# Loading 128 rows of wo first, halving w_down's first loads, and storing y with one DMA, in a one-token decode kernel

## The chip, the cores and the metric

The kernel runs on one core of a Trainium2 chip. The metric is the device time of one execution in microseconds (us), the median of several runs, so lower is better. A profiled execution also gives a span, from its first to its last instruction, which is about 2 us shorter than the run's time. All positions below, such as "at 287.5", are microseconds from the start of that span. In the profile lines PE is TensorE and PEld its weight loads, DVE is VectorE, ACT ScalarE, POOL GpSimd and SP SyncE; SPq and ACTq are the instruction sequencers of SyncE and ScalarE, and q1, q8, q10 and q14 are queues of transfers.

## The reference

One decoded token for a batch of two: attention over the last 2048 of 8192 cached keys, then a gated feed-forward block. Everything is bf16.

```python
B, D, Hq, Hkv, Sk, Dh, F = 2, 640, 32, 32, 8192, 192, 1536
W = min(4096, max(256, Sk // 4))                       # 2048
q = (layernorm(x) @ wq)                                # 32 heads of 192
k, v = k_cache[:, :, Sk - W:, :], v_cache[:, :, Sk - W:, :]
o = softmax(q @ k.T * Dh ** -0.5) @ v                  # per batch row and head
h = x + o.reshape(B, 1, Hq * Dh) @ wo
hn = layernorm(h)
y = h + (gelu(hn @ w_gate) * (hn @ w_up)) @ w_down
```

Every input byte that is needed is read once: 100.66 MB of K and V, 7.86 MB each of wq and wo, 5.90 MB of w_gate, w_up and w_down. That is the 122.29 MB that the profile counts on SyncE's queue. The output is 2,560 bytes.

## The kernel before

All large loads go out on SyncE's queue, in the order in which they are needed, into one ring of on-chip memory. A load waits only until the part of the ring that it overwrites has been read. ScalarE's queue carries x at the start and half of the result at the end.

```python
WDC = ((0, 3), (3, 6), (6, 9), (9, 11), (11, 12))   # w_down: five loads, of 3, 3, 3, 2, 1 row groups
...
    P.op("sp", lambda e, v=v, src=src: e.dma_start(v, src), W=toks + [("sem", sem)], dma=sem)   # every ring load
...
def load_wo(J):                                     # four quarters of wo, the last one in two parts
    src = A_wo[1536 * J:1536 * (J + 1), :].rearrange("(p kk) n -> p kk n", kk=12)
    for i, (k0, k1) in enumerate(wo_parts(J)): ...
def wo_parts(J):
    return ((0, 12),) if J < 3 else ((0, 8), (8, 12))
...
P.op("act", lambda e: e.dma_start(xrow[0:2, :], A_x[:, 0, :]), W=["xrow"], dma="dx")
load_k(0); load_wq(); load_k(1); ...                # then v0, k2, v1, ..., wo quarters between,
load_wo(2); load_wo(3); load_ffn()                  # w_gate, w_up in two parts, w_down in five
```

The tail of the arithmetic:

```python
# w_gate and w_up: four column blocks side by side on the PE, contiguous columns
    e.matmul(bank[32*r:32*r+2, 0:384], lhsT=hnT[:, c, :], rhs=wv[:, c-c0, 384*r:384*(r+1)], ...)
...
gT = ffn_columns(grow, "grow", tps[0], 0)
pe(h_rows, ...)                                     # puts h into the accumulator of y
... # gelu of the gate on DVE and ScalarE, w_up, product -> uT
for i, (f0, f1) in enumerate(WDC):                  # w_down, group by group as it lands
    e.matmul(m1[32*r:32*r+2, 0:160], lhsT=uT[:, f, :], rhs=wd[:, f-f0, 160*r:160*(r+1)], ...)
dve(lambda e: e.tensor_copy(yrow[0:98, :], m1[0:98, 0:160]), ...)
for b, q in ((0, "sp"), (1, "act")):                # result: one store for each batch row, on two queues
    P.op(q, lambda e, b=b: e.dma_start(out[b, 0, :].rearrange("(r n) -> r n", r=4), yrow[b:b+97:32, :]), ...)
```

SyncE waits for both stores; then the program ends.

## Time and profile before

| | before |
|---|---|
| median of the first 3 runs | 294.56 us (294.52 to 294.61) |
| profiled span | 292.5 us |
| SyncE's queue q1 | 98.0% of 16 engines' span |
| last w_down load, first / mean / last of its 16 completions | 287.45 / 288.44 / 289.52 |
| stores issued, later one complete | 290.27, 292.12 |

The two bottom rows come from the records of single transfers. A load is spread over 16 transfer engines and completes once on each, so "first" and "last" are the fastest and the slowest engine. The prediction quotes the page's rates, the windows at both ends and the chain of waits. Here is what it uses but doesn't print: first the page's line of busy engines and its line of packets.

```profile
PE 192.4 (66%) x2141; PEld 149.2 (51%) x2141; DVE 128.0 (44%) x310; ACT 96.0 (33%) x120; POOL 8.4 (3%) x35
DMA packets 6654, 122.44 MB, mean 419 GB/s; under 512 B 754, under 2 KB 884, under 8 KB 1652
```

PE, the busiest engine, works 66% of the span; 122.44 MB is what all queues move together, instructions included. Then lines of the timeline (start, duration, engine, source line, operation, tiles, count; in brackets how long the engine was idle before, and what ended that).

```profile
0.74 0.56 ACTq L406 DMA_DIRECT2D xrow<-in_A_x_dram  x1
0.74 0.65 SPq L343 DMA_DIRECT2D ring<-in_A_k_cache_dram  x1
...
280.64 1.77 PE L780 MATMUL sps<-ring,hnT 128*2 128x384 bf16 x20 [0.79 <-DVE hnT L404]
...
283.76 0.71 PE L797 MATMUL m<-hrow,hsel 98*2 98x160 f32 x8
...
284.25 1.82 PE L780 MATMUL ops<-ring,hnT 128*2 128x384 bf16 x20
...
287.46 0.18 DVE L404 TENSOR_TENSOR uT<-tps,ga 128x24 bf16<-128x24 f32 x1 [1.73 <-PE tps L789]
```

Both queues issue their first load at the same moment. The 20 matmuls of w_gate take 1.77 us, the h_rows matmuls (L797) stand right before those of w_up, and uT, which every w_down matmul needs, starts to be written at 287.46.

### The profile page before, as it was taken

Reading aid. Unit: us, or ns where it says so; the run is one execution under the profiler, and the core shown is the slowest. Engines: PE = TensorE matmul, PEld = TensorE weight load, DVE = VectorE, ACT = ScalarE, POOL = GpSimd, SP = SyncE. Lnnn points to the kernel's source line nnn. Section 1 sums busy time; section 2 is a strip of 40 time slices with the busy share of each in tenths; the row PEclk is TensorE's granted clock in tenths of the full one; section 3 lists DMA queues with packets and bytes.
Section 4 is the critical chain, followed back from the end, with each engine's and each line's share of the span. In section 5 each row is a group of like instructions: output and inputs, shape, how many; then the busy total and the mean of one; then the engine's idle time right before and its main releaser. Section 6 shows DMA issues by size and latency. Waiting matters only on the chain.

```text
span 292.5 us, 5066 instructions
## 1 busy us (share of the span) xinstructions
PE 192.4 (66%) x2141; PEld 149.2 (51%) x2141; DVE 128.0 (44%) x310; ACT 96.0 (33%) x120; POOL 8.4 (3%) x35
## 2 busy tenths in 40 slices
PE   2450858848678198849495596658696856586665
PEld 1440436718475195628282575456565653563432
DVE  5950085623437154516155255426265454162331
ACT  2150115623432143616152144324343443341000
POOL 3000020000000000000000000000000000000000
PEclk9996699995979579988879599959797999597955
DMA  7998999999999999999999999999999999999993
GB/s 283 450 497 351 429 437 432 430 432 430 429 415 441 430 430 428 430 430 430 430 412 446 430 430 434 430 430 430 430 430 430 430 430 430 430 430 409 429 404 151
DMA packets 6654, 122.44 MB, mean 419 GB/s; under 512 B 754, under 2 KB 884, under 8 KB 1652
## 3 DMA queue, kind: packets, MB, share of 16 engines
q1 hardware_dynamic: 6632, 122.29, 98.0%
q8 instruction: 7, 0.11, 0.2%
q14 instruction: 3, 0.02, 0.0%
q10 hardware_dynamic: 12, 0.00, 0.0%
HBM read 122.29 MB, written 0.00 MB: 418 GB/s over the span
## 4 chain that ended last, share of the span: by engine, by line
DMA 75%; PE 20%; SPq 3%; DVE 1%; issue 0%
DMA ring<-in_A_k_cache_dram 57%; PE tps L551 15%; DMA ring<-in_A_wq_dram 10%; DMA ring<-in_B_w_down_dram 8%; SPq L343 3%; PE tps L572 2%; PE ops L653 1%; PE m L704 1%; PE m L686 1%; DVE ktr L563 0%; DVE ering L404 0%; PE m L826 0%; PE m L637 0%; PE m L667 0%; DVE yrow L832 0%
## 5 line engine op out<-in xcount | busy, mean ns | idle before, releaser
L551 PE MATMUL tps<-identf,ring 128*128 128x128 f32 x768 | 112.7, 314 | 46.6 <-DMA ring<-in_A_k_cache_dram 45.3
L551 PEld LDWEIGHTS tps<-identf,ring 128*128 128x128 f32 x768 | 104.1, 164 | 50.2 <-DMA ring<-in_A_k_cache_dram 46.6
L560 ACT ACTIVATE ktr<-tps 128x1024 bf16<-128x1024 bf16 x80 | 79.2, 1023 | 83.6 <-PE tps L551 83.6
L563 DVE COPY ktr<-tps 128x1024 bf16<-128x1024 bf16 x112 | 74.2, 688 | 72.2 <-PE tps L551 71.5
L628 ACT ACTIVATE eexp<-sm,nm 128x512 bf16<-128x512 f32 x16 | 11.5, 721 | 65.0 <-DVE nm L626 65.0
L653 PE MATMUL ops<-ring,ering 128*32 128x384 bf16 x512 | 24.9, 339 | 5.4 <-DMA ring<-in_A_v_cache_dram 5.4
L617 DVE CUSTOM_DVE_ANT_1 sm<-sps,mska 128x512 f32<-128x512 f32 x16 | 11.1, 691 | 35.7 <-PE sps L609 35.7
L609 PE MATMUL sps<-ktr,rq 128*16 128x512 bf16 x384 | 24.6, 389 | 1.1 <-POOL rq L404 1.1
L653 PEld LDWEIGHTS ops<-ring,ering 128*32 128x32 bf16 x512 | 12.8, 99 | 14.1 <-DMA ring<-in_A_v_cache_dram 6.7
L609 PEld LDWEIGHTS sps<-ktr,rq 128*16 128x16 bf16 x384 | 9.2, 88 | 11.4 <-POOL rq L404 1.2
L624 PEld LDWEIGHTS m<-mrhs,pm 128*128 128x128 bf16 x16 | 1.5, 96 | 23.5 <-DVE mrhs L400 23.5
L624 PE MATMUL m<-mrhs,pm 128*128 128x16 bf16 x16 | 2.9, 183 | 15.7 <-DVE mrhs L400 15.7
L572 PE MATMUL tps<-ring,xnT 128*32 128x384 bf16 x80 | 5.6, 464 | 11.0 <-DMA ring<-in_A_wq_dram 11.0
L404 POOL TENSOR_TENSOR rq<-qs,mask 128x96 bf16<-128x96 bf16 x16 | 5.6, 360 | 195.4 <-PE sps L609 161.3
L572 PEld LDWEIGHTS tps<-ring,xnT 128*32 128x32 bf16 x80 | 3.1, 132 | 13.3 <-issue 11.2
L595 DVE CAST qs<-ops 128x384 bf16<-128x384 f32 x1 | 0.6, 558 | 17.6 <-PE ops L590 17.6
L404 DVE TENSOR_TENSOR ering<-m,mask 128x256 bf16<-128x256 f32 x16 | 6.7, 418 | 1.9 <-PE m L637 1.7
L456 ACT ACTIVATE lt<-m,eps_t 128x2 f32<-128x2 f32 x2 | 0.5, 262 | 19.4 <-PE m L454 19.4
L579 ACT ACTIVATE qrow<-tps 128x768 bf16<-128x768 f32 x1 | 0.8, 810 | 15.6 <-PE tps L572 15.6
L637 PE MATMUL m<-sel,eexp 128*128 128x64 bf16 x64 | 4.6, 196 | 1.2 <-ACT eexp L628 1.2
L404 DVE TENSOR_TENSOR orow<-m,wm 128x1536 bf16<-128x1536 f32 x3 | 5.3, 1751 | 0.0
L704 PE MATMUL m<-ring,ot 128*2 128x320 bf16 x96 | 4.1, 298 | 1.6 <-DMA ring<-in_A_wo_dram 1.6
(115 smaller groups left out, 86.5 us busy)
## 6 DMA issues: line engine op xcount, KB each, us to landing
ring<-in_A_k_cache_dram SPq DMA_DIRECT2D x16, 3072.0 KB, 31.7
ring<-in_A_v_cache_dram SPq DMA_DIRECT2D x16, 3072.0 KB, 27.3
ring<-in_A_wq_dram SPq DMA_DIRECT2D x1, 7680.0 KB, 28.2
ring<-in_A_wo_dram SPq DMA_DIRECT2D x3, 1920.0 KB, 19.2
ring<-in_B_w_gate_dram SPq DMA_DIRECT2D x1, 1920.0 KB, 32.0
ring<-in_B_w_up_dram SPq DMA_DIRECT2D x1, 1536.0 KB, 24.3
ring<-in_B_w_down_dram SPq DMA_DIRECT2D x3, 480.0 KB, 26.4
ring<-in_A_wo_dram SPq DMA_DIRECT2D x1, 1280.0 KB, 26.8
```

The costliest lines, as they stand in the source:

```text
L343: P.op("sp", lambda e, v=v, src=src: e.dma_start(v, src), W=toks + [("sem", sem)], dma=sem)
L404: return lambda e: e.tensor_tensor(out=out, in0=a, in1=b, op=op)
L551: ins = e.transpose(tps[bi][:, 128 * u:128 * (u + 1)], kv[:, off:off + 128], identf[:, :])
L560: act(lambda e, dst=dst, bv=bv: e.activation(out=dst, in_=bv, func=ACT.Copy), W=[("kt", n)], X=[("t", bi)])
L563: dve(lambda e, dst=dst, bv=bv: e.tensor_copy(dst, bv), W=[("kt", n)], X=[("t", bi)], cls=0)
L572: ins = e.matmul(tps[0][32 * r:32 * (r + 1), 0:384], lhsT=xnT[:, c, 32 * J:32 * (J + 1)], rhs=wq[:, c, 1536 * J + 384 * r:1536 * J + 384 * ...
L609: ins = e.matmul(sps[32 * ch:32 * ch + 16, :], lhsT=rq[:, g % 4, k, :], rhs=ktr[:, k // 2, 1024 * ch + k % 2:1024 * (ch + 1):2], start=(k ...
L617: dve(lambda e: e.tensor_tensor_reduce(out=sm[:, :].rearrange("p (u x) -> p u x", u=4), in0=sps[:, :].rearrange("p (u x) -> p u x", u=4), ...
L628: act(lambda e: e.activation(out=eexp[:, :], in_=sm[:, :], func=ACT.Exp, bias=nm[:, 0:1], scale=1.0, accum_out=zr[:, g % 4:g % 4 + 1]), R= ...
L637: ins = e.matmul(o, lhsT=eexp[:, 128 * u:128 * (u + 1)], rhs=sel64[:, :], start=True, stop=True)
L653: ins = e.matmul(ops_[32 * r:32 * (r + 1), 0:384], lhsT=ering[:, g % 4, t, :], rhs=vv[:, 384 * t:384 * (t + 1)], start=(g % 4 == 0 and t < 4),
L704: ins = e.matmul(m1[32 * r:32 * r + 2, 192:512], lhsT=ot[:, kk, :], rhs=wo[:, kk - k0, 320 * h:320 * (h + 1)], start=(kk == 1 or J < 2 and ...
```

## The change

The intent is to shorten the stream of transfers at its two ends. While SyncE's queue starts up, ScalarE's queue already fetches the last 128 rows of wo, which then need not be loaded near the end. w_down needs one load fewer, with larger packets. And the result leaves in one DMA of 8 rows. The larger w_down rows alter which row of w_down stands on which partition, so w_gate's and w_up's columns are read with a stride; and for one store the two batch rows must lie on partitions 16 apart, so the stationary operand becomes 17 columns wide.

```diff
-WDC = ((0, 3), (3, 6), (6, 9), (9, 11), (11, 12))
+WDC = ((0, 6), (6, 9), (9, 11), (11, 12))
+WOE = 6016
 ... (new tile wosp; wider ot, hsel and uT)
 def load_wo(J):
-    src = A_wo[1536 * J:1536 * (J + 1), :].rearrange("(p kk) n -> p kk n", kk=12)
+    nk = 12 if J < 3 else 11
+    src = A_wo[1536 * J:1536 * J + 128 * nk, :].rearrange("(p kk) n -> p kk n", kk=nk)
-    return ((0, 12),) if J < 3 else ((0, 8), (8, 12))
+    return ((0, 12),) if J < 3 else ((0, 8), (8, 11))
 ... (w_down read as "(q p s) n -> q p s n" with s=6)
+P.op("act", lambda e: e.dma_start(wosp[32:96, :, :], A_wo[WOE:, :].rearrange("(p j) n -> p j n", j=2)), W=["wosp"], dma="dsp")
 P.op("act", lambda e: e.dma_start(xrow[0:2, :], A_x[:, 0, :]), W=["xrow"], dma="dx")
 ... (two memsets on POOL: all of uT, and wosp[0:32])
 ... (oproj(3): four matmuls of wosp, ahead of the wait for the rest of that quarter)
-    rhs=wv[:, c - c0, 384 * r:384 * (r + 1)]
+    cols = wv[:, c - c0, 768 * (r // 2):768 * (r // 2 + 1)].rearrange("p (x s) -> p x s", s=6)
+    rhs=cols[:, :, 3 * (r % 2):3 * (r % 2) + 3]
+pe(h_rows, ...)
 gT = ffn_columns(grow, "grow", tps[0], 0)
-pe(h_rows, ...)
-    m1[32 * r:32 * r + 2, 0:160], lhsT=uT[:, f, :]
+    m1[32 * r:32 * r + 17, 0:160], lhsT=uT[:, f, 0:17]
-dve(lambda e: e.tensor_copy(yrow[0:98, :], m1[0:98, 0:160]), W=["y"], X=["m1"])
-for b, q in ((0, "sp"), (1, "act")):
-    P.op(q, lambda e, b=b: e.dma_start(out[b, 0, :].rearrange("(r n) -> r n", r=4), yrow[b:b + 97:32, :]),
-         R=["y"], W=[("out", b)], dma=f"dout{b}")
+dve(lambda e: e.tensor_copy(yrow[0:113, :], m1[0:113, 0:160]), W=["y"], X=["m1"])
+P.op("act", lambda e: e.dma_start(out[:, 0, :].rearrange("b (r n) -> r b n", r=4), yrow[0:113:16, :]), R=["y"], W=["out"],
+     dma="dout")
```

## The prediction

> **What bounds the kernel now.** I read the page from part 2 down. It says first whether the transfers ever stop.
>
> ```profile
> DMA  7998999999999999999999999999999999999993
> q1 hardware_dynamic: 6632, 122.29, 98.0%
> q8 instruction: 7, 0.11, 0.2%
> DMA 75%; PE 20%; SPq 3%; DVE 1%; issue 0%
> ```
>
> The first line cuts the 292.5 us span into 40 slices and shows the transfer engines at 90% or more in all but the first slices and the last. SyncE's queue (q1) alone fills 98.0% of the span on all 16 engines and moves 122.29 MB; the last line, the chain of waits, is three quarters transfer. Away from the ends the rate is steady at about 430 GB/s. The PE is 66% busy and is not the bound. So the end is set by **start of the transfers + bytes over rate + what follows the last landing**. To move it, a change has to move one of those three.
>
> The start and the end need a finer view. This is a table of short stretches, with the DMA share and GB/s in the last two columns:
>
> ```profile
> 1.60:1.70 0.10, 0.00 (x0) 0.00 (x0) 0.04 (x1) 0.10 (x1) 0.10 (x2) 1.00 0.04 13
> 2.00:2.10 0.10, 0.00 (x0) 0.00 (x0) 0.10 (x1) 0.10 (x1) 0.10 (x1) 1.00 0.00 0
> 2.10:2.20 0.10, 0.00 (x0) 0.00 (x0) 0.10 (x1) 0.10 (x1) 0.10 (x1) 1.00 3.55 983
> 287.00:288.00 1.00, 0.72 (x15) 0.42 (x17) 0.18 (x1) 0.00 (x0) 0.00 (x0) 0.50 0.66 240
> 288.00:289.20 1.20, 1.11 (x36) 0.73 (x32) 0.00 (x0) 0.00 (x0) 0.00 (x0) 0.50 0.33 126
> ```
>
> A packet is booked where it starts, hence 3.55 and 983. ScalarE's tiny load of x starts moving at 1.68 us, but the first packets of K, issued at the same moment, start only at 2.16 to 2.58 us. There is an almost empty half microsecond at the front. At the back the share falls from 1.0 to 0.66 and 0.33: the 16 engines don't finish together. The trace has one completion per engine; those of the last w_down load run from 287.45 to 289.52 us, so the slowest engine, 2.07 us behind the first, sets the end. Then the chain of waits closes with:
>
> ```profile
> 265.46 23.65 DMA ring<-in_B_w_down_dram
> 289.12 0.04 issue
> 289.16 0.73 PE m L826 x12
> 289.89 0.02 issue
> 289.92 0.32 DVE yrow L832
> ```
>
> The PE was idle for 0.44 us before row groups 9 and 10 and for 0.30 us before group 11, both times waiting for w_down: the arithmetic is ahead of the loads at the end. After that, in the order of time:
>
> ```profile
> 290.27 0.66 SPq L834 DMA_DIRECT2D out_dram<-yrow  x1
> 290.27 0.61 ACTq L834 DMA_DIRECT2D out_dram<-yrow  x1
> ```
>
> The store issued by ScalarE completes at 291.94, the one by SyncE at 292.12; SyncE waits for both and the span ends 0.4 us later.
>
> **What the Trainium skill says.** (1) "DMA: Bandwidth & Descriptors", section "Issuing engines are not separate DMA queues": loads issued from ScalarE and SyncE run on the same 16 engines and interleave. So the second queue buys no bandwidth. The trace agrees that a single queue already fills the engines (98.0%). (2) Same page, section "The descriptor swizzle": partitions map to engines in blocks of four, with the halves 0-63 and 64-127 on engines 0-7 and 8-15. Partitions 32-95 in 16 shares of four then follow that same map, which explains the odd range. No run here shows it yet. (3) "SBUF — State Buffer", section "Door 1: The DMA port swizzle (why `[64,N]` ≈ `[32,N]`)": strided reads are free while at least two of the accesses fall in one 16-byte line, 8 bf16 apart at most. The new reads of w_gate and w_up take 3 columns of every 6, so about 4 per line, and should be free; the trace before has only contiguous ones there. (4) "Runtime: NRT & Kernel Launch", section "Instruction fetch mechanics": instructions are refilled in 16 KiB blocks. The trace agrees: seven packets of 16384 bytes on q8, about 1 us each, which compete with the loads.
>
> **The change, part by part.**
>
> *128 rows of wo first.* 128 x 640 x 2 bytes = 0.164 MB. At 430 GB/s that is **0.38 us** of all engines; per engine 4 packets of 2560 bytes, which took about 0.10 us each where w_down uses this size. The bytes leave the second part of the last wo load (landing at 275.50 us) and everything behind it moves up by 0.38 us, minus what K and all later loads are delayed by at the start. The total of bytes is the same, so the gain is only what fits in the front gap. ScalarE's load should start near 1.7 to 1.9 us and needs 0.4 us, so it would be done at 2.1 to 2.5, when K starts. The first K packets took 1.26 to 1.80 us against 0.91 later, so there is more slack in them. I choose 0.25 us as the part that is hidden (0 if the queues are served in turn, 0.38 if all is). x now comes second on ScalarE, perhaps a microsecond later, but the q projection waits for wq until 29.63 us: no cost.
>
> *w_down's first half in one load.* 8 packets of 7680 bytes per engine instead of 16 of 3840, and 16 semaphore packets of 9 ns fewer in all. A 3840-byte packet took about 148 ns, which is 26 bytes/ns against 27 for 24576 bytes: at most 8 x 6 ns, so **0.05 us**. Its landing is that of the former second load, at 287.15, before uT at 287.69: no new wait.
>
> *Arithmetic of the tail.* The four early wo matmuls fill a wait for wo (0.83 us idle), and 6 column steps remain for the last part instead of 8: 0.1 us less. The h_rows matmuls (0.49 us between their start at 283.76 and that of w_up's at 284.25) move into the copy of grow, in which the PE idles for 0.66 us. So uT comes about 0.1 + 0.49 us earlier, and further with the wo landing; w_up's own landings at 283.76 and 284.74 may hold back some of it. Against that stands the wider stationary operand (17 columns for 2). The PE at the same half clock ran four 384-column matmuls in 320 ns with 2 columns and also with 32, so this is free. All of it is worth **0** at the end, because the PE already waits there for w_down; it only makes room.
>
> *One store.* Four destination rows bound the spread, so again 4 engines, now 2 packets each of about 19 ns. If it takes ScalarE's former 1.67 us from issue to completion and not SyncE's 1.85, **0.1 to 0.18 us** fall away. The copy of 113 partitions costs as much as that of 98.
>
> *Added.* Two memsets on POOL, which is 3% busy: nothing.
>
> Sum: 0.25 + 0.05 + 0.12 = 0.42 us. 294.56 - 0.42 = **294.1 us**, 0.14% faster.
>
> **Rivals.** *Hidden anyway, or a wash*: if K's first packets wait for ScalarE's descriptors, the 0.38 us are only moved from the back to the front and only the store's 0.1 is left: 294.4. For it: K started in two groups, eight engines at 2.16 and eight at 2.5, as if descriptors are written one after the other. Against it: x started half a microsecond ahead. *The PE becomes the bound of the tail*: if 3-of-6 strided reads ran at half speed, 40 matmuls that take 3.6 us would take 7.2 us, uT would come at about 290.5, and 2 us of matmuls would follow, so the end moves by some 2.5 us to 297. At a quarter of the speed it passes 2%. Against it: scores read every second column at a pace of 64 ns per 512 columns shared four ways, near full rate. *The slowest engine changes*: the 2.07 us between engines come partly from instruction blocks; a few instructions more or less can put one block on another engine, worth about 0.6 us (16384 bytes at 27 bytes/ns) either way.
>
> **Range and chances.** The three small terms give 293.95 to 294.5; the slow-engine rival widens it. I take **293.6 to 294.8**. 2% would be 5.9 us. The transfers' 122 MB are untouched, so faster by that much is all but impossible (0.005); slower needs the strided reads to be four times slower (0.015); within 2% gets 0.98.
>
> **What would show each step.** Right: the first transfers start before 2.0 us and K's first load still completes at about 10.3 to 10.9; the second wo part and all w_down parts land 0.25 to 0.4 us earlier; PE still waits for w_down before its last groups; uT is written before 287.2; the single store completes 1.7 us after issue. Wrong: K's first completion at 10.7 or later (a wash); 20 matmuls of w_gate in clearly more than 1.8 us, or no PE wait before w_down's last groups (PE bound); a spread between the first and last engine far from 2.07 us (slow engine).

## The result, and the profile after

| | before | after |
|---|---|---|
| median | 294.56 us (6 runs, 294.32 to 294.61) | 294.32 us (6 runs, 294.02 to 294.54) |
| profiled span | 292.5 | 292.5 |
| first K load, first to last completion | 10.34 to 10.91 | 10.79 to 11.19 |
| last w_down load, first / mean / last | 287.45 / 288.44 / 289.52 | 287.51 / 288.39 / 289.62 |
| issue of the store to its last completion | 1.85 | 1.73 |

The ratio is 0.9992, with a 95% interval of 0.9980 to 1.0005. All ratios here divide the mean time of one kernel's fast runs by that of the other's fast runs of the same rounds, so they are not quite the ratios of the medians. The profiled execution of the changed kernel happened to be the slowest of its six runs (294.54), so equal spans say nothing against the small gain.

The page of the changed kernel, the lines that answer to those of before in the prediction (q1 and q10 are SyncE's and ScalarE's loads; q14, like q8 in the prediction, brings pieces of the program):

```profile
DMA packets 6586, 122.44 MB, mean 419 GB/s; under 512 B 750, under 2 KB 880, under 8 KB 1584
q1 hardware_dynamic: 6480, 122.13, 97.8%
q10 hardware_dynamic: 96, 0.17, 0.1%
q14 instruction: 3, 0.02, 0.0%
DMA 77%; PE 19%; SPq 2%; DVE 1%; issue 0%
```

0.16 MB have moved from q1 to q10, the sum of the bytes is the same, and the chain is still three quarters transfer. Next the table of short stretches (stretch, its length, then the busy time of PE, PEld, DVE, ACT and POOL, granted clock, DMA share and GB/s):

```profile
1.60:2.10 0.50, 0.00 (x0) 0.00 (x0) 0.44 (x3) 0.00 (x0) 0.50 (x2) 1.00 0.00 0
2.10:2.20 0.10, 0.00 (x0) 0.00 (x0) 0.10 (x1) 0.00 (x0) 0.10 (x1) 1.00 2.03 492
...
287.00:288.00 1.00, 0.69 (x21) 0.54 (x24) 0.22 (x1) 0.00 (x0) 0.00 (x0) 0.50 0.56 219
288.00:289.20 1.20, 1.02 (x28) 0.36 (x16) 0.00 (x0) 0.00 (x0) 0.00 (x0) 0.50 0.33 120
```

The half microsecond at the front that was to be filled is now wholly empty: nothing moves before 2.1. At the back the rate fades as it did before. The timeline shows why ScalarE's load isn't in that gap, and how the tail stands:

```profile
0.74 0.63 SPq L345 DMA_DIRECT2D ring<-in_A_k_cache_dram  x1
0.75 0.66 ACTq L409 DMA_DIRECT2D wosp<-in_A_wo_dram  x1
1.44 0.92 ACTq L410 DMA_DIRECT2D xrow<-in_A_x_dram  x1
...
280.81 1.77 PE L805 MATMUL sps<-ring,hnT 128*2 128x384 bf16 x20 [0.79 <-DVE hnT L407]
282.39 0.73 PE L822 MATMUL m<-hrow,hsel 98*17 98x160 f32 x8
284.02 0.10 PEld L805 LDWEIGHTS ops<-ring,hnT 128*2 128x2 bf16 x8 [0.32 <-DMA ring<-in_B_w_up_dram]
...
287.19 0.22 DVE L407 TENSOR_TENSOR uT<-tps,ga 128x24 bf16<-128x24 f32 x1 [1.29 <-PE tps L814]
...
289.25 0.12 PEld L851 LDWEIGHTS m<-ring,uT 128*17 128x17 bf16 x8 [0.55 <-DMA ring<-in_B_w_down_dram]
289.66 0.10 PEld L851 LDWEIGHTS m<-ring,uT 128*17 128x17 bf16 x4 [0.29 <-DMA ring<-in_B_w_down_dram]
290.03 0.33 DVE L857 CAST yrow<-m 113x160 bf16<-113x160 f32 x1 [2.62 <-PE m L851]
290.39 0.67 ACTq L858 DMA_DIRECT2D out_dram<-yrow  x1
```

ScalarE issued its load 0.01 us after SyncE. In the records of single packets, its first packet starts at 5.49 us, although it was issued at 0.75. From there each transfer engine takes one K packet of 24,576 bytes (0.912 us), one wo packet of 2,560 bytes (0.102 us), the next K packet and so on: the wo packets start near 5.5, 6.5, 7.5 and 8.5, and the load is complete at 9.88 to 10.28. The view of DMA issues (queue, count, size, microseconds from issue to landing) says the same in one line:

```profile
wosp<-in_A_wo_dram ACTq DMA_DIRECT2D x1, 160.0 KB, 9.5
```

The first K load ends 0.28 to 0.45 us later than before, which is what four packets of 0.102 us cost each engine. At the end of the tail the PE waits for w_down as before, and the chain closes with:

```profile
261.31 27.90 DMA ring<-in_B_w_down_dram
289.26 0.75 PE m L851 x11
290.03 0.33 DVE yrow L857
```

So the first question is whether the early wo rows gained nothing at all. The second is where the 0.2 us that the medians show come from. The third is what holds the slowest engine two microseconds back.

### The profile page after: what moved, and what is told of

Its sections match the earlier page's. It is cut to its first block, busy times and chain, and to the rows that moved or that the text cites. A ratio compares the mean times of both kernels' runs of the same rounds, so it can differ in the third digit from the quotient of the medians.

```text
span 292.5 us, 5073 instructions
## 1 busy us (share of the span) xinstructions
PE 194.5 (66%) x2144; PEld 152.3 (52%) x2144; DVE 128.4 (44%) x310; ACT 96.2 (33%) x120; POOL 9.2 (3%) x37
## 4 chain that ended last, share of the span: by engine, by line
DMA 77%; PE 19%; SPq 2%; DVE 1%; issue 0%
DMA ring<-in_A_k_cache_dram 57%; PE tps L558 15%; DMA ring<-in_A_wq_dram 10%; DMA ring<-in_B_w_down_dram 10%; SPq L345 2%; PE tps L579 1%; PE ops L660 1%; PE m L728 1%; PE m L696 1%; DVE ktr L570 0%; DVE ering L407 0%; PE m L851 0%; PE m L644 0%; PE m L674 0%; DVE yrow L857 0%
## 5 line engine op out<-in xcount | busy, mean ns | idle before, releaser
L558 PE MATMUL tps<-identf,ring 128*128 128x128 f32 x768 | 116.5, 321 | 46.8 <-DMA ring<-in_A_k_cache_dram 41.5
L558 PEld LDWEIGHTS tps<-identf,ring 128*128 128x128 f32 x768 | 108.1, 169 | 49.9 <-DMA ring<-in_A_k_cache_dram 42.7
L570 DVE COPY ktr<-tps 128x1024 bf16<-128x1024 bf16 x112 | 74.2, 688 | 75.1 <-PE tps L558 74.3
L644 PEld LDWEIGHTS m<-sel,eexp 128*128 128x128 bf16 x64 | 4.4, 105 | 1.6 <-DVE nm L633 1.3
L670 DVE COPY osb<-ops 128x192 f32<-128x192 f32 x8 | 2.5, 354 | 6.0 <-PE ops L660 6.0
L696 PE MATMUL m<-selb,orow 128*128 128x2 bf16 x47 | 3.4, 199 | 1.9 <-DVE ering L407 1.6
```

Of the source, the lines that this page charges most:

```text
L558: ins = e.transpose(tps[bi][:, 128 * u:128 * (u + 1)], kv[:, off:off + 128], identf[:, :])
L570: dve(lambda e, dst=dst, bv=bv: e.tensor_copy(dst, bv), W=[("kt", n)], X=[("t", bi)], cls=0)
L644: ins = e.matmul(o, lhsT=eexp[:, 128 * u:128 * (u + 1)], rhs=sel64[:, :], start=True, stop=True)
L696: ins = e.matmul(m2[:, 2 * kk:2 * kk + 2], lhsT=of[:, kk:128 * nk:nk], rhs=selb[:, :], start=True, stop=True)
```

## The experiments

**Theory A**: the early wo rows are a wash, because the same bytes are only moved from the back of the full stream to its front; the gain is that of the single store. **Theory B**: the front gap can be filled and the changed kernel only lost a race, 0.01 us between the two queues; where ScalarE asks first, 0.25 us or more are to be had. **Theory E**, beside these: the end is set by one late transfer engine, and instruction blocks (pieces of the program, which come by the same transfers, in packets of 8 or 16 KB) make it late, so a few instructions more or less could mask or feign such gains. The expectations use the same letters. Their C and D, under sp_second, are two guesses about the race of theory B: by C the queue that asks first is served first, by D ScalarE's load starts late whoever asks first.

Four kernels shared one chip and one set of runs of the kernel before (294.61 us, 9 runs).

### after_again: the change as it is

No edit. It is the yardstick of its group.

> The changed kernel once more, as the base for the others on the same chip. Theory A (the early rows of wo are not hidden: their packets take turns with K's on every engine): first K load complete at about 10.8 to 11.2 us instead of 10.3 to 10.9, last w_down landing within 0.2 us of the kernel before, time 0.1 to 0.3 us below it, from the single store and chance. Theory B (hidden in the front gap, as predicted): last w_down landing 0.3 us earlier, time 0.4 us below before.

Measured: 294.42 us (294.09 to 294.67), ratio 0.9991 (0.9978 to 1.0005). The last w_down load completes at 287.56 / 288.47 / 289.60, the store 1.74 us after its issue. The first result repeats in a second set of runs.

### wo_home: the change without its first part

```diff
-nk = 12 if J < 3 else 11          # load_wo, o_columns
+nk = 12
-... else ((0, 8), (8, 11))
+... else ((0, 8), (8, 12))
-P.op("act", lambda e: e.dma_start(wosp[32:96, :, :], ...))   # with its memset and its four matmuls
```

> The changed kernel with the 128 rows of wo loaded where they were, in the last wo load; all other parts kept. Theory A: the first K load completes 0.3 to 0.4 us earlier than in the changed kernel, but the last w_down landing and the time are the same within 0.1 us, since the bytes only moved. Theory B: 0.25 us slower than the changed kernel.

Measured: 294.38 us (294.30 to 294.56), ratio 0.9993 (0.9979 to 1.0007). The first K load is back at 10.26 to 10.75, and the last w_down load is at 287.38 / 288.33 / 289.51. Without the early wo rows the kernel is as fast as with them (294.42). That is theory A's number. By their scatter, five runs each leave about a quarter of a microsecond open either way, so the landings are the better sign: over all profiles of this case without added instructions, the mean landing of the last w_down load is 288.30 to 288.47 in the five whose early rows come on ScalarE's queue, and 288.33 to 288.44 in the three that load them at the end.

### no_wo_rows: those bytes not loaded at all

The result is wrong: the 128 rows are taken as zeros. (The check of the result, with these inputs, does not notice 128 rows of wo.)

```diff
-P.op("act", lambda e: e.dma_start(wosp[32:96, :, :], A_wo[WOE:, :]...), W=["wosp"], dma="dsp")
-pool(lambda e: e.memset(wosp[0:32, ...], 0), W=["wosp0"])
+pool(lambda e: e.memset(wosp[0:128, ...], 0), W=["wosp0", "wosp"])
```

> The changed kernel without the load of the 128 rows at all (zeros instead; the result is wrong on purpose). Theory A: the 0.164 MB cost 0.38 us on the stream, so the last w_down landing and the time fall by 0.38 us against the changed kernel. Theory B: the load was hidden in the front gap, so taking it away changes less than 0.15 us.

Measured: 293.95 us (293.91 to 294.17), ratio 0.9980 (0.9966 to 0.9993). The chain of waits of this kernel ends with:

```profile
260.62 27.91 DMA ring<-in_B_w_down_dram
288.58 0.74 PE m L850 x11
289.35 0.33 DVE yrow L856
```

Its last matmuls stand 0.68 us before those of the changed kernel's chain (289.26 to 288.58). That pair of profiles shows the largest difference: against after_again, of the same chip, the mean landing of the last w_down load is 0.55 us earlier (288.47 to 287.92), the median 0.47, and by the ratios it is 0.32 (0.0011 of 294.6). Against wo_home, which loads the same bytes at the end, the median is 0.43 us lower. The estimate from the bytes was 0.38, in the midst of these. So bytes that are truly left out give their price back, and in the changed kernel, within this scatter, that price is paid in full.

### two_stores: the result in two DMAs again

```diff
-P.op("act", lambda e: e.dma_start(out[:, 0, :].rearrange("b (r n) -> r b n", r=4), yrow[0:113:16, :]), ...)
+for b, q in ((0, "sp"), (1, "act")):
+    P.op(q, lambda e, b=b: e.dma_start(out[b, 0, :].rearrange("(r n) -> r n", r=4), yrow[16 * b:16 * b + 97:32, :]), ...)
```

> The changed kernel with the result stored by two DMAs of four rows again, from SyncE and ScalarE. If the single store saves time: completion of the later store 1.85 us after issue instead of 1.73, and the kernel 0.1 us slower than the changed one. If it saves nothing: both complete 1.7 us after issue and the time is the same.

Measured: 294.73 us (294.57 to 294.99), ratio 1.0005 (0.9992 to 1.0019): the gain is gone, 0.31 us against after_again. Its timeline:

```profile
290.23 0.66 SPq L859 DMA_DIRECT2D out_dram<-yrow  x1
290.24 0.63 ACTq L859 DMA_DIRECT2D out_dram<-yrow  x1
```

They are issued together, and complete at 292.18 (SyncE's, after 1.95 us) and 291.90 (ScalarE's, after 1.67 us). The later one decides. Here the issue stood 0.13 us earlier than in after_again, and the span still ended 0.14 us later.

The next three shared another chip (before: 294.63 us, 11 runs).

### sp_second: ScalarE asks first

SyncE's first K load waits for a small memset on POOL, so that ScalarE is certainly ahead.

```diff
+pool(lambda e: e.memset(gate[:, :], 0), W=["gate"])
-P.op("sp", ..., W=toks + [("sem", sem)], dma=sem)
+P.op("sp", ..., R=["gate"] if key == ("k", 0) else [], W=toks + [("sem", sem)], dma=sem)
```

> The changed kernel with SyncE's first K load held back until a one-element memset of POOL is done, some 0.2 us, so that ScalarE asks for its transfer first. Theory C (the queue that asks first is served first): the rows of wo start moving before 2.1 us instead of at 5.5 and complete before 3.5 us instead of at 10; K's first packets start 0.2 us later; the last w_down landing is 0.1 to 0.3 us earlier than in the changed kernel. Theory D (ScalarE's 64 descriptors come late whoever asks first): the rows still start at about 5 us, and the time is 0.2 us worse.

Measured: 294.44 us (294.42 to 294.50), ratio 0.9993 (0.9980 to 1.0006). Its timeline and its DMA issue:

```profile
0.73 0.09 POOL L410 MEMSET gate<- 1x1 int32 x1 [0.29 <-POOLq L906]
0.75 0.67 ACTq L411 DMA_DIRECT2D wosp<-in_A_wo_dram  x1
0.85 0.63 SPq L346 DMA_DIRECT2D ring<-in_A_k_cache_dram  x1
```

```profile
wosp<-in_A_wo_dram ACTq DMA_DIRECT2D x1, 160.0 KB, 3.2
```

Now the wo rows do come first: their packets start at 2.21 us and are complete at 3.04 to 3.90. But they start no earlier than K's did, and K's first packets move to between 2.70 and 3.55. The first K load completes at 10.74 to 11.18, as in the changed kernel, and the last w_down load at 287.56 / 288.41 / 289.52, not the 0.1 to 0.3 us earlier that C expected. D fails too: the rows do not start at 5 us here. Theory B falls: the race is not what cost the gain.

### wo_on_sp: the wo rows on SyncE's own queue, ahead of K

```diff
-P.op("act", lambda e: e.dma_start(wosp[32:96, :, :], ...), W=["wosp"], dma="dsp")
+P.op("sp", lambda e: e.dma_start(wosp[32:96, :, :], ...), W=["wosp"], dma="dsp")
```

> The changed kernel with the 128 rows of wo loaded by SyncE's own queue ahead of K. One queue keeps its order, so the rows move first, at about 2.1 us, and complete by 4 us. K is asked for 0.6 us later and its first packets start at about 2.7 to 3.1 us. If K's start is all that counts: last w_down landing 0.2 to 0.3 us later than in the changed kernel, less if the rows fill the gap ahead of K. x lands at about 2.1 us again.

Measured: 294.56 us (six runs, 294.17 to 295.79), ratio 1.0005 (0.9992 to 1.0018). One run, at 295.79, stands apart from the other five, all at 294.60 or less; the one profile is that of the 294.17 run, so it cannot explain it. The DMA issue:

```profile
wosp<-in_A_wo_dram SPq DMA_DIRECT2D x1, 160.0 KB, 2.7
```

Its packets start at 2.16 us and K's between 2.84 and 3.63. The first K load completes at 11.02 to 12.24, and the last w_down load at 287.79 / 288.75 / 289.56: in the mean 0.36 us later than in the changed kernel, as expected, but on the slowest engine no later. With one queue alone the front gap stays. It belongs to every load of these runs that is spread over all 16 engines: in all twelve profiles the first such load, issued at 0.74 or 0.75 us, moves its first packet at 2.14 to 2.21 us, whether it is 3 MB of K or 0.16 MB of wo. What started earlier in the kernel before was only x, of two packets. So none of the loads tried here can be placed ahead of another in that time, because the time is its own start-up. Whether the 16 engines or the number of packets (64 and 128, against two) make it longer than that of x, no run separates.

### more_code, and its repair more_code3: instruction blocks on purpose

Theory E was tested by giving POOL more instructions than it needs, without more data. The first attempt appended dependent memsets:

```diff
+for i in range(1024):
+    pool(lambda e: e.memset(gate[:, :], 0), W=["gate"])
```

> The changed kernel with 1024 one-element memsets added on POOL after its last useful instruction (some 205 to 240 us): 64 KiB more instructions to fetch, nothing else. Theory E (each instruction block is moved by one of the 16 engines, which then stays behind the others to the end, and the slowest engine sets the end): four to eight more blocks in the trace, each followed by one more engine behind, and the last completion of w_down 0.5 to 1.5 us later; time up by as much. Rival: blocks are spread over all engines or caught up: at most 0.15 us (64 KiB at 430 GB/s).

Measured: 356.85 us, ratio 1.2115 (1.2097 to 1.2132). This is a flaw of the experiment: each memset waited for the one before, 147 ns apart, and 1024 of them took 150 us and outlasted the kernel. Only its inner part can be read: the last w_down load completed at 287.59 to 290.87, a spread of 3.28 us where the changed kernel has 2.11, and the store was complete at 293.31, 1.2 us late. A second build (more_code2), with independent memsets to columns of one partition, was refused before any run: two of POOL's cores, one with an earlier instruction and one with these memsets, could have written the same 16 partitions at once. The third has 640 of them on another partition, and POOL is done at 229 us:

```diff
+for i in range(640):
+    pool(lambda e, i=i: e.memset(wosp[0:1, 0, i:i + 1], 0), W=["wosp0"] if i == 639 else [])
```

> As more_code, but 640 independent memsets, so that POOL is done long before the end and the time itself can be read: 40 KiB more instructions on an idle engine. Theory E (an instruction block puts one transfer engine behind for good, and the slowest engine sets the end): about five more 8192-byte blocks; if one of them falls on an engine that is already behind, the last completion of w_down is 0.3 to 1.2 us later than in the changed kernel and the time is up by as much; if all fall on engines that were ahead, the mean lag rises and the last does not. Rival: blocks are caught up or spread: last and mean within 0.1 us.

Measured, on a further chip (before: 294.54 us, 9 runs): 295.90 us (295.55 to 296.07), ratio 1.0046 (1.0032 to 1.0059). The page's instruction queue and POOL's slices:

```profile
POOL 4000100000000000000000000001978200000000
...
q14 instruction: 8, 0.07, 0.1%
```

The changed kernel has this q14 line with 3 packets. Five more blocks, 40 KiB or 0.03% of all bytes, cost 1.36 us against the kernel before, and 1.6 us if the 0.08% that the change gains elsewhere is counted. At 430 GB/s they would be 0.1 us of all engines. The timeline at the end:

```profile
290.40 0.11 PEld L853 LDWEIGHTS m<-ring,uT 128*17 128x17 bf16 x8 [0.59 <-DMA ring<-in_B_w_down_dram]
...
291.47 0.67 ACTq L860 DMA_DIRECT2D out_dram<-yrow  x1
```

The PE waits for the same load as in the changed kernel, 1.15 us later. The 16 completions of every load give the history of the slowest engine. This is its distance behind the fastest one:

| kernel | after the event | slowest engine behind by |
|---|---|---|
| before | first K load | 0.57 us |
| before | 8 KB block at 16.97 | 1.15 |
| before | 16 KB block at 34.68 | 1.75 |
| before | 16 KB block at 50.48 | 2.25, then 2.11 |
| before | last w_down load | 2.07 |
| more_code3 | load landed at 208.11 | 1.97 |
| more_code3 | 8 KB blocks at 208.49, 213.71, 218.94 | 1.99 to 2.06 |
| more_code3 | 8 KB blocks at 224.16, 229.38 | 3.36 |
| more_code3 | last w_down load | 3.25 |

In the kernel before, each later 16 KB block (61.4, 75.1, 90.8 us) puts one more engine over 1 us behind; in the end 7 of 16 are over 1.4 us behind. In more_code3 three of the five added blocks leave the slowest engine where it was, and the last two go with its step of 1.3 us; the mean lag of all engines rises only from 0.85 to 1.08 us. Summed over the 16 engines, the lag in the kernel before grows by 1.25 to 1.57 us at each of six 16 KB blocks and by 0.78 to 1.12 us at each of three 8 KB blocks. That is more than the packets themselves take, 1.00 to 1.10 and 0.31 to 0.33 us; why, no run tells. The lag is never made up in more_code3 and hardly in the kernel before, where the queue leaves no engine a pause in which it could be. That instruction blocks put single engines behind, and that this moves the end, is therefore shown. Which engine each block falls on is not named in the trace; it was inferred from which completion, in the order of their lags, steps back.

The last two shared one more chip (before: 294.53 us, 9 runs).

### store_only: the kernel before with the single store and nothing else

```diff
-hsel = sb("hsel", [128, 2, B], F32);  uT = sb("uT", [128, NF, B], BF16)
+hsel = sb("hsel", [128, 2, 17], F32); uT = sb("uT", [128, NF, 18], BF16)      # and a memset of uT
... (17-column operands, yrow[0:113], the single store of the change)
```

> The kernel before with the single store alone (and the 17-column operands that it needs); wo, w_down and h_rows stay as they were. If the store is the whole gain: its completion 1.65 to 1.75 us after issue instead of 1.85 for the later of two, the time 0.2 to 0.3 us below the kernel before and within 0.1 us of the changed kernel. If the early wo rows or the merged w_down load carry part of the gain: less than 0.1 us.

Measured: 294.36 us (294.08 to 294.52), ratio 0.9993 (0.9979 to 1.0007), with the store complete 1.71 us after its issue. As far as these runs resolve it, the whole measured gain of the change is there in this part alone. The timeline also bears on what the moved h_rows matmuls do for the changed kernel:

```profile
287.68 0.22 DVE L404 TENSOR_TENSOR uT<-tps,ga 128x24 bf16<-128x24 f32 x1 [1.76 <-PE tps L790]
287.96 1.82 PE L827 MATMUL m<-ring,uT 128*17 128x160 bf16 x48 [0.31 <-DVE uT L404]
289.46 0.10 PEld L827 LDWEIGHTS m<-ring,uT 128*17 128x17 bf16 x4 [0.19 <-DMA ring<-in_B_w_down_dram]
```

uT comes 0.49 us later than in the changed kernel (287.19), all 48 matmuls run in one piece, and the PE has only one wait left, of 0.19 us. With some 0.2 us more delay of uT (an estimate from that wait) the PE would set the end. The 0.49 us are not all owed to h_rows: in the eight profiles without added instructions in which it is moved, the write of uT starts anywhere from 286.40 to 287.45, against 287.46 and 287.68 in the two in which it is not.

### store_sp: the single store on SyncE

```diff
-P.op("act", lambda e: e.dma_start(out[:, 0, :]..., yrow[0:113:16, :]), ...)
+P.op("sp", lambda e: e.dma_start(out[:, 0, :]..., yrow[0:113:16, :]), ...)
```

> The changed kernel with the single store issued by SyncE instead of ScalarE. If the two stores of before hinder each other (one waits for the other): SyncE's alone takes 1.65 to 1.75 us too, and the time is that of the changed kernel. If SyncE's way to a store is the slower one: 1.85 us or more, and the time 0.1 to 0.2 us above the changed kernel.

Measured: 294.34 us (294.00 to 294.44), ratio 0.9988 (0.9974 to 1.0001). The store in its timeline:

```profile
290.19 0.69 SPq L858 DMA_DIRECT2D out_dram<-yrow  x1
```

Alone on SyncE it takes 1.72 us from issue to completion, so SyncE's queue is not slower; 1.85 and 1.95 us were the price of two stores at once. In all ten profiles with a single store it takes 1.71 to 1.74 us. By chance ScalarE won the race at the start of this profiled run: the wo rows landed 2.7 us after their issue, and the time is that of the other kernels, as in sp_second.

No kernel here with the right result clearly beats the changed one. store_only, wo_home and the change agree within their scatter, and store_only is the simplest of them.

## Why the prediction was right or wrong

The time was predicted as 294.1 us, in 293.6 to 294.8, within 2%. It came out as 294.32, in the range and in that class. The range also held the old time, 294.56, so this alone confirms little. The bound was read rightly: a stream that never stops, and an end set by its last landing. The sum was 0.42 us, the medians differ by 0.24; one term of it failed.

- **Early wo rows, 0.25 us "as the part that is hidden": this step failed.** It gave 0. The step held that ScalarE's load "should start near 1.7 to 1.9 us". It started at 5.49, and, asked first, at 2.16 to 2.21. x's early start misled: x is two packets, and its start-up (0.94 us from issue to first packet) is not that of a load spread over 16 engines (1.42 us). The text named the other outcome, "0 if the queues are served in turn", and they are. The Trainium skill says so on the page that the prediction had open, "DMA: Bandwidth & Descriptors", section "Queues, rings and completion order": "each SDMA engine round-robins between the queue rows it has work for, at *packet* granularity". The trace agrees, with its turns of 0.912 and 0.102 us. The rival "a wash" is what happened, and its sign too, K's first completion at 10.7 us or later: it was 10.79. Its figure, 294.4, was the better one.
- **x "perhaps a microsecond later": wrong in size, right in effect.** x landed at 11.22 us after 2.09 before. The q projection waits for wq until 30.18 us, so it costs nothing.
- **w_down in one load less, 0.05 us: not seen.** store_only (five loads, ratio 0.9993) and wo_home (four, 0.9993) can't be told apart. 0.05 us is below what five runs resolve. The text's sum counts 8 packets where 16 of 3840 bytes go, so its own figures allow 0.1 us at most. In the records a packet of 7680 bytes took 295 ns against 149 to 152 for one of 3840, which makes 0.02 to 0.07 us for eight.
- **One store, "0.1 to 0.18 us": right, but for another reason, and if anything too small.** The records give 0.12 us in the first pair (1.85 to 1.73) and 0.21 in the second (1.95 to 1.74), the medians 0.17 (store_only against before) and 0.31 (two_stores against after_again; the means of those five runs each differ by 0.36, with an interval of about 0.06 to 0.65 worked out from their scatter). The text put the longer time down to SyncE; store_sp shows that the second store was the cause. Each single interval but that of no_wo_rows and the code experiments includes 1. The verdict rests on the repetition: of seven pairings of a single-store kernel with the kernel before, six give 0.9988 to 0.9993, and only wo_on_sp, with its stray run, 1.0005. (The seven share four sets of runs of the kernel before, so they are not seven independent tests.) two_stores, the only variant of the change with two stores, gives 1.0005.
- **The PE's tail, 0 at the end: right.** The strided w_gate matmuls take 1.77 us as before, the 17-column ones cost nothing that shows, and PE still waits 0.55 and 0.29 us for w_down. uT was to be "written before 287.2"; its write began at 287.19 and ended at 287.41, since w_up's landing held the PE (0.32 us at 284.02), as the text allowed.
- **The slow-engine rival: real, and mis-sized.** The spread at the end stayed the same (2.07 and 2.11 us); both kernels have 7 blocks of 16 KB and 3 of 8 KB. But "about 0.6 us" for a 16 KB block is too little: each added 1.25 to 1.57 us of lag in the kernel before, and five blocks of 8 KB made 1.36 us of the whole time.

Two things stay open. Why ScalarE's first packet waited until 5.49 us in the changed kernel, some three K packets per engine after K's first (4.59 in two_stores, where SyncE came first as well), no run tells. Nor is it shown that the scatter of half a microsecond between the runs of one kernel comes from blocks falling on different engines, though it would fit.

## What to carry to other kernels

When one queue already fills the transfer engines, moving bytes to another queue or to another time gains nothing unless the engines truly stand idle then; look at the start of a load of the same kind before calling a gap free. At the end of this kernel one store that covers all rows beat two issued at once on two queues, by about 0.2 us. And in a kernel bound by transfers, the size of the instruction stream counts: a block puts an engine back, and where that one becomes the slowest, the end moves with it.

## What the Trainium skill lacked or had wrong

- "Runtime: NRT & Kernel Launch", section "Instruction fetch mechanics", says of the cost of a block boundary: "one DMA tail-bump, mostly hidden". For the fetching engine no run contradicts it, but the blocks travel on the same 16 transfer engines as the data. Five blocks of 8 KB on q14 (the page knows only blocks of 16 KiB) made the kernel 1.36 us slower, and in the kernel before the slowest engine goes from 0.57 to 2.07 us behind.
- "DMA: Bandwidth & Descriptors", section "Queues, rings and completion order", has queues taking turns by packets of "≈9-17 descriptors typical". Here the turn passed after every single record of 24,576 bytes, one partition's row of K (0.912 us); how many descriptors stand behind one record the trace does not say. A load of 0.16 MB took 9.5 us to land, against 2.7 to 3.2 us where it asked first.
- Same page, section "Latency and other measured facts", gives about 600 ns to the first byte for this kind of DMA, but not the moment from which it counts, nor any dependence on the load. Here, from the start of the issuing instruction, it was 0.94 us for a load of two packets and 1.40 to 1.46 us for one spread over 16 engines; from that instruction's end 0.38 us, and 0.77 to 0.82 us.
- No page has what two small stores issued at once cost each other: the later one completes after 1.85 and 1.95 us, one alone after 1.71 to 1.74 us on either queue.
